# Gated linear attention and MLP on one core: decay rows stored with head pairs innermost, g loaded as rows, first q scaled ahead of k

## The chip, the cores and the metric

The kernel runs on one core of a Trainium2 chip. The core has a matrix engine (TensorE, PE in the profile, with PEld for its weight loads), a vector engine (VectorE, DVE), an activation engine (ScalarE, ACT), a general engine (GpSimd, POOL) and SyncE (SP), which here does little but issue DMAs. Each engine runs its own list of instructions in order and waits on semaphores for the others. The metric is device time in microseconds (us) from launch to end; smaller is better.

## The reference

The inputs are q, k, v and alpha, each with 4 batches, 8 heads, 768 tokens and 48 features per head, and the MLP's g_ln, w_ch1 and w_ch2. The first half is a recurrence per head:

```python
for t in range(S):
    state = alpha[:, :, t, :, None] * state + np.einsum('bhd,bhe->bhde', k[:, :, t], v[:, :, t])
    y[:, :, t] = np.einsum('bhd,bhde->bhe', q[:, :, t], state)
```

The heads are then laid side by side into rows of 384, and the second half is an MLP with a residual:

```python
xn = (x - mu) / np.sqrt(var + 1e-06) * g_ln
out = x + np.maximum(xn @ w_ch1, 0.0) @ w_ch2
```

w_ch1 is 384 x 1536 and w_ch2 1536 x 384, both given as 8-byte floats, which the kernel rounds to 4 bytes itself.

## The kernel before, in words

The 768 tokens are cut into 6 chunks of 128. For each chunk c and batch b, `attention(c, b)` replaces the loop over tokens by matrix products. With L the running sum of log(alpha) within a block, q is multiplied by exp(L) and k by exp(-L); the scores are then an ordinary masked product of q and k, and the state is carried from block to block by a factor exp(L at the block's last token), one number per head and feature. The code calls these factors the gates. In chunk 0 a block is the whole 128 tokens (one row of gates), later it is a half of 64 (two rows).

The steps of one `attention`, with the names of the profile:

- L341, ACT: `la` = Ln(alpha). L346 (chunk 0) and L353 (later), PE: `lps` = running sum, a product with a triangle of ones from `consts`.
- L356, ACT: `eq` = Exp(lps). L357, ACT: `lps` = Exp(-lps), in place.
- L359, DVE: the k half of `qk` = k * lps. L361, DVE: the q half of `qk` = q * eq.
- L367, SP: the last row (or the two last rows) of `eq` goes to a DRAM tile `row`, 512 numbers a row. L461, SP: `row` is read back into `gate`, so that the numbers of one row lie one below the other, feature by partition, with one column for each of the 4 pairs of heads. L479 (DVE, chunk 0) and L485 (POOL, later) multiply the state by `gate`.
- L413, PE: `qk` is transposed, k first, then q (from step 12 of 24 on a DVE block transpose and DMAs do it instead); L417 copies. L426/L441, PE: scores `aps`. L450/L455, DVE: masked copy into `at`. L470, PE: `ups`, the update of the state. L496/L506, PE: outputs `yps`.
- L515 to L566: layer norm without g, and its transpose `xT`.

In `eq` of before, the free order is pair of heads, head of the pair, feature (64 places, 48 used): `[P, NP, 2, 64]`. A row in DRAM has that order too, so in the read at L461 the 4 pairs of one feature lie 128 numbers apart:

```python
nc.sync.dma_start(gate[:, :ne], row[:ne].rearrange("o (p r) -> r o p", p=NP))
```

The MLP: `g_ln` is folded into w_ch1. Each of 8 weight pieces is staged (`ws`) and rounded by `round_weights`: DVE L250, L252, L254, then ACT L256, then DVE L260, and for w_ch1 three L263, which multiply by the column `g_col` of `small`. For the first piece ACT also scales `g_col` by 2^-20 (L258). `g_col` is loaded by an ACT-issued DMA (L220) from g_ln, viewed as 128 partitions by 3 columns. Chunk 0 goes through the plain products L589 (`hidden`) and L601 (`project`); chunks 1 to 5 through products of sums of blocks (L892, L713), whose sums DVE and POOL make (L695, L836, L861, L666 and others).

The order of all this is written out by hand: each attention step, weight piece, product and sum is a generator, and `ORDER` (L28) is a string of letters, each of which advances one generator by one `yield` (L963). Instructions go to the engines in exactly that order; nothing reorders them. The DMAs of SP go out in their order too, and SP stops at a DMA that must wait. Before the string begins there are loads of `consts` (ACT) and alpha (SP), memsets, and 8 matmuls on zeros (L286) in a PSUM bank named `idle`.

Of the kernel before, what the change touches and what calls it, by code (L numbers as in the profile page):

```python
# [9 lines left out]
FP32 = mybir.dt.float32  # L10
# [4 lines left out]
AOP = mybir.AluOpType  # L15
# [40 lines left out]
def pick(marks, usual=0):  # L56
    return int(marks.pop(0)) if marks else int(usual)
# [3 lines left out]
def kernel(  # L61
# [36 lines left out]
    nc = tc.nc  # L98

    B, S, H, D = q.shape  # L100
    DM = H * D
    DF = w_ch1.shape[1]
    P = 128
    NCB = S // P
    NP = H // 2
    R = 64 + D
    NF = DM // P
# [4 lines left out]
    cpool = ctx.enter_context(tc.tile_pool(name="const", bufs=1))  # L112
# [11 lines left out]
    r = np.arange(P)  # L124
# [3 lines left out]
    raws = {}  # L128
# [80 lines left out]
    tri, ident = consts[:, :P], consts[:, P:2 * P]  # L209
# [8 lines left out]
    w2_src = w_ch2.rearrange("(j p) m -> p j m", p=P)  # L218
    with nc.allow_non_contiguous_dma(reason="one small column load"):
        nc.scalar.dma_start(g_col, g_ln.rearrange("(f p) -> p f", p=P))  # L220

    pieces = []
# [16 lines left out]
    def round_weights(i):  # L239
# [11 lines left out]
           op0=AOP.bitwise_and, op1=AOP.bitwise_or)  # L251
# [4 lines left out]
        nc.scalar.activation(out=lo, in_=lo, func=AFT.Relu, scale=8.0, bias=least)  # L256
        if i == 0:
            nc.scalar.mul(g_col, g_col, 2.0 ** -20)  # L258
        yield
# [21 lines left out]
    more = cpool.tile([P, 4, NJ // 3 * DM // 2], FP32, name="more")  # L281
    zero = more.rearrange("p i m -> p (i m)")[:, 20 * P:21 * P]
    nc.vector.memset(zero, 0.0)
    idle = ps.tile([P, 512], FP32, name="lps", tag="bank", bufs=6)
    for _ in range(8):
# [6 lines left out]
    shared = more.rearrange("p i m -> p (i m)")[:, :4 * NP * P]  # L292
    eqs = [cpool.tile([P, NP, 2, 64], FP32, name=f"eq{b}") for b in range(2)]
    eqs += [shared[:, i * NP * P:(i + 1) * NP * P].rearrange(
        "p (a b c) -> p a b c", b=2, c=64) for i in range(2)]
    qks = [cpool.tile([P, 2, NP, 2, 64], FP32, name=f"qk{b}") for b in range(3)]
    qks.append(shared[:, 2 * NP * P:].rearrange("p (i a b c) -> p i a b c", i=2, b=2, c=64))
    sts = [[cpool.tile([R, NP, D], FP32, name=f"st{b}_{i}") for i in range(2)] for b in range(B)]
    for b in range(B):
        nc.vector.memset(eqs[b].rearrange("p a b c -> p (a b) c")[:, :, D:], 0.0)  # L300
        nc.vector.memset(qks[b].rearrange("p i a b c -> p (i a b) c")[:, :, D:], 0.0)
# [3 lines left out]
    def eq_of(c, b):  # L305
        return eqs[b if c < 2 else b % 2]
# [11 lines left out]
    for u in updates:  # L318
        nc.vector.memset(u, 0.0)

    x_of, xT_of, hT_of, las, turned_of, scores = ({} for _ in range(6))

    def attention(c, b):
# [12 lines left out]
        qk = qk_of(c, b).rearrange("t n p i c -> t n i p c")[:, :, :, :, :D]  # L338
        eq = eq_of(c, b).rearrange("t p i c -> t i p c")[:, :, :, :D]
        la = work.tile([P, 2, NP, D], FP32, name="la", tag="row", bufs=8)  # L340
# [7 lines left out]
        else:  # L348
# [9 lines left out]
        yield  # L358
        nc.vector.tensor_mul(qk[:, 1], raws.pop(("k", c, b)), lv)  # L359
        yield  # L360
        (nc.vector, nc.gpsimd)[pick(marks)].tensor_mul(  # L361
            qk[:, 0], raws.pop(("q", c, b)), eq)
        ends = slice(P - 1, P) if whole else slice(HS - 1, P, HS)
        ne = 1 if whole else 2
        row = dram.tile([2, 2 * 64 * NP], FP32, name="row", tag="row")
        gate = work.tile([P, 2, NP], FP32, name="gate", tag="gate", bufs=B)
        nc.sync.dma_start(row[:ne], eq_of(c, b)[ends].rearrange("o p i c -> o (p i c)"))  # L367
        yield
# [91 lines left out]
        with nc.allow_non_contiguous_dma(reason="two rows to columns"):  # L460
            nc.sync.dma_start(gate[:, :ne], row[:ne].rearrange("o (p r) -> r o p", p=NP))  # L461
        yield
# [157 lines left out]
    def buffers_of_last():  # L620
# [7 lines left out]
        late_of["h"] = [t.rearrange("p (j b t) -> p j b t", b=HB, t=P) for t in h]  # L628
        sums = [t.rearrange("t p i c -> t (p i c)") for t in eqs[:2]]
        sums += [more_x[:, NT * HB * P:]] + [t[:, 512:] for t in free]  # L630
# [363 lines left out]
```

## Time and profile before

| | |
|---|---|
| median of 3 runs | 419.09 us (417.46 to 420.03) |
| profiled execution | 418.39 us |
| its span, first to last instruction | 416.6 us |
| PE busy | 410.1 us, 98% |
| DVE, ACT, POOL busy | 292.3, 217.3, 120.4 us |
| mean share of the 16 DMA engines, SP's queue | 56.7% |
| DMA packets, and those under 512 B | 134445, 90956 |
| L361 q * eq, L356 Exp, each 24 times | 0.55 and 0.49 us each |

The profile is of one execution; the 1.8 us between its time and its span lie outside the first and last instruction. "PE busy" includes the time in which a matmul is stretched by the next one's wait, so 98% is not a peak; the chain of waits tells which engine the end hangs on. A row of the timeline gives start, duration, engine, line, what is written and read, and in brackets how long the engine was idle before it and who ended that. In a table by windows, each engine has its busy time and its number of instructions, followed by the granted clock, the DMA share and the GB/s.

### The profile page before, as it was taken

The page shows a single profiled execution, that of the slowest core. Times are in us where ns is not written, and L with a number is a line of the kernel's source. Part 1 is how long each engine was busy: PE and PEld are TensorE (multiplying, and loading weights), DVE is VectorE, ACT ScalarE, POOL GpSimd, SP SyncE. Part 2 cuts the span into 40 slices and gives each one's busy share as a digit, 9 for nine tenths or more (in the row PEclk, how much of TensorE's full clock was granted, in tenths as well). Part 3 has the DMA queues.
Part 4 walks back from the last instruction along what each step waited for, and adds up shares of the span by engine and source line. Part 5 has one row for each costly group of instructions (what it writes and reads, how often), then busy time and mean ns, then how long its engine had stood idle before and what let it go on. Part 6 is the DMA issues. An engine that isn't in the chain of part 4 may idle for free.

```text
span 416.6 us, 11452 instructions
## 1 busy us (share of the span) xinstructions
PE 410.1 (98%) x4616; PEld 355.0 (85%) x4616; DVE 292.3 (70%) x554; ACT 217.3 (52%) x522; POOL 120.4 (29%) x134
## 2 busy tenths in 40 slices
PE   7999999999999999999999999999999999999997
PEld 5887888876568789998889998899998889999996
DVE  4797989998997878688268983579533298115754
ACT  4798568773364577245585335873353643245110
POOL 1011023130011562144470254260236321525300
PEclk9999999999999999999999999999999999999999
DMA  7998968788878576945767758636323200000301
GB/s 249 289 258 258 298 155 289 206 196 211 245 156 240 154 133 141 244 100 121 186 135 160 191 160 211 116 61 132 108 57 119 72 1 2 19 0 23 111 20 57
DMA packets 134445, 61.26 MB, mean 147 GB/s; under 512 B 90956, under 2 KB 131276, under 8 KB 134392
## 3 DMA queue, kind: packets, MB, share of 16 engines
q1 hardware_dynamic: 133848, 60.37, 56.7%
q8 instruction: 36, 0.59, 0.6%
q10 hardware_dynamic: 544, 0.17, 0.2%
q14 instruction: 17, 0.14, 0.1%
HBM read 43.12 MB, written 17.39 MB: 145 GB/s over the span
## 4 chain that ended last, share of the span: by engine, by line
PE 94%; DMA 2%; DVE 1%; ACT 1%; issue 1%; SPq 0%; DVEq 0%
PE hps L892 32%; PE ops L713 31%; PE hps L589 8%; PE ops L601 8%; PE yps L506 5%; PE aps L441 3%; PE tps L413 2%; PE ups L470 2%; PE lps L353 2%; DMA ra<-in_alpha_dram 2%; PE aps L426 1%; PE yps L496 1%; DVE eq L861 1%; PE xps L564 1%; SPq L166 0%
## 5 line engine op out<-in xcount | busy, mean ns | idle before, releaser
L892 PE MATMUL hps<-sum,w 128*128 128x256 f32 x192 | 46.3, 383 | 0.0
L892 PEld LDWEIGHTS hps<-sum,w 128*128 128x128 f32 x192 | 35.6, 190 | 6.3 <-ACT u L904 1.7
L713 PE MATMUL ops<-w,hT 128*128 128x192 f32 x224 | 40.5, 326 | 0.0
L737 ACT COPY u<-ops 128x192 f32<-128x192 f32 x30 | 9.5, 317 | 54.3 <-PE ops L713 54.2
L713 PEld LDWEIGHTS ops<-w,hT 128*128 128x128 f32 x224 | 37.3, 190 | 0.3
L733 POOL TENSOR_TENSOR ob<-ob,u 128x192 f32<-128x192 f32 x32 | 20.4, 648 | 57.3 <-ACT u L737 33.0
L485 POOL TENSOR_TENSOR mid<-mid,gate 112x192 f32<-112x192 f32 x20 | 13.2, 660 | 79.5 <-DMA gate<-row 47.5
L589 PE MATMUL hps<-xT,w 128*128 128x256 f32 x144 | 33.9, 385 | 0.2 <-ACT few L537 0.2
L892 PE MATMUL hps<-xT,w 128*128 128x256 f32 x136 | 33.3, 380 | 0.6 <-DVE xT L861 0.6
L904 ACT COPY u<-hps 128x512 f32<-128x512 f32 x32 | 18.7, 586 | 28.6 <-PE hps L892 22.4
L601 PE MATMUL ops<-w,hT 128*128 128x384 f32 x96 | 32.6, 491 | 0.0
L589 PEld LDWEIGHTS hps<-xT,w 128*128 128x128 f32 x144 | 26.2, 190 | 4.2 <-ACT few L537 0.4
L904 ACT COPY hT<-hps 128x512 f32<-128x512 f32 x40 | 23.3, 586 | 12.3 <-PE hps L892 11.9
L892 PEld LDWEIGHTS hps<-xT,w 128*128 128x128 f32 x136 | 25.7, 190 | 4.3 <-PE ops L713 0.9
L713 PE MATMUL ops<-ws,sum 128*128 128x192 f32 x160 | 28.6, 327 | 0.0
L601 PEld LDWEIGHTS ops<-w,hT 128*128 128x128 f32 x96 | 17.7, 190 | 11.7 <-issue 0.6
L713 PEld LDWEIGHTS ops<-ws,sum 128*128 128x128 f32 x160 | 26.4, 190 | 0.7 <-ACT few L537 0.6
L727 DVE TENSOR_TENSOR ob<-ops,ob 128x192 f32<-128x192 f32 x40 | 13.1, 350 | 16.9 <-PE ops L713 10.4
L931 ACT ACTIVATE hT<-hT 128x512 f32<-128x512 f32 x40 | 22.9, 621 | 2.0 <-DVE hT L911 1.5
L713 PE MATMUL ops<-ws,hT 128*128 128x192 f32 x128 | 23.4, 326 | 0.0
L713 PE MATMUL ops<-more,sum 128*128 128x192 f32 x120 | 22.2, 328 | 0.0
L713 PEld LDWEIGHTS ops<-ws,hT 128*128 128x128 f32 x128 | 21.3, 190 | 0.1
(223 smaller groups left out, 1029.3 us busy)
## 6 DMA issues: line engine op xcount, KB each, us to landing
ws<-in_moe_w_ch_dram SPq DMA_DIRECT2D x8, 1152.0 KB
vn<-in_v_dram SPq DMA_DIRECT2D x12, 384.0 KB
kept<-x SPq DMA_DIRECT2D x24, 192.0 KB
ob<-kept SPq DMA_DIRECT2D x24, 192.0 KB
rows<-rj SPq DMA_DIRECT2D x48, 96.0 KB
out_dram<-ob SPq DMA_DIRECT2D x18, 192.0 KB
xrows<-xt SPq DMA_DIRECT2D x64, 48.0 KB
xT<-xrows SPq DMA_DIRECT2D x16, 192.0 KB
```

Source lines behind the costliest of these rows:

```text
L441: nc.tensor.matmul(pair[o][halves[i if o else 1 - i], p, s], k_of[rs, p, s], q_of[rs, p, s], start=True, stop=True)
L485: nc.gpsimd.tensor_mul(new, new, by)
L506: nc.tensor.matmul(yps[j][halves[s], i, p], of, by, skip_group_check=True, start=not (cross and k), stop=k == 1 or not cross)
L589: nc.tensor.matmul(hps, w1[:, f, j * P:(j + 1) * P], xT_of[0][:, f, bs], start=(f == 0), stop=(f == NF - 1))
L601: nc.tensor.matmul(ops_of[b], hT_of[c][:, j, b], w2[:, j], start=(j == 0), stop=(j == NJ - 1))
L713: nc.tensor.matmul(acc, lhs[:, j], rhs[:, j], start=j == 0 and n not in FOLLOWS, stop=j == NT - 1 and n not in FOLLOWS.values(), skip_grou ...
L727: nc.vector.tensor_add(x, acc, x)
L733: getattr(nc.vector if c + 1 == NCB else nc.gpsimd, f"tensor_{op}")(x, x, y)
L737: copy(out=copied[n], in_=acc)
L892: nc.tensor.matmul(acc[:, i], w, b, start=n not in JOINS and i == 0, stop=n not in JOINS.values(), skip_group_check=True)
L904: nc.scalar.copy(out=copied[n], in_=acc)
L931: nc.scalar.activation(out=x, in_=x, func=AFT.Relu)
```

## The change

There are three edits.

1. `eq` is laid out as `[P, 2, 64, NP]`: the 4 pairs of heads are innermost. Exp (L356) writes it with a step of 4 numbers between features, and the q product (L361) reads it so. The row in DRAM has the same order, and the read into `gate` takes the 4 pairs of a feature as 16 consecutive bytes. The built program has `gate<-row` as 128 x 4 (chunk 0) and 128 x 2 x 4 (later), where before it was 128 x 4 x 1 and 128 x 8 x 1.
2. g_ln is loaded as 3 rows of 128 into a free part of `more`, transposed on PE into the `idle` bank, and copied to `g_col` by a DVE instruction, which also does the scaling by 2^-20. The column load and the ACT instruction L258 are gone.
3. In the first attention step alone, q * eq is issued on DVE ahead of k * lps.

```diff
-    with nc.allow_non_contiguous_dma(reason="one small column load"):
-        nc.scalar.dma_start(g_col, g_ln.rearrange("(f p) -> p f", p=P))
...
-        if i == 0:
-            nc.scalar.mul(g_col, g_col, 2.0 ** -20)
...
+    g_row = more.rearrange("p i m -> p (i m)")[:NF, 21 * P:22 * P]
+    nc.scalar.dma_start(g_row, g_ln.rearrange("(f p) -> f p", p=P))
     nc.vector.memset(zero, 0.0)
...
-    eqs = [cpool.tile([P, NP, 2, 64], FP32, name=f"eq{b}") for b in range(2)]
+    eqs = [cpool.tile([P, 2, 64, NP], FP32, name=f"eq{b}") for b in range(2)]
...
+    nc.tensor.transpose(idle[:, P:P + NF], g_row, ident[:NF, :NF])
+    nc.vector.tensor_scalar(out=g_col, in0=idle[:, P:P + NF], op0=AOP.mult, scalar2=None,
+                            scalar1=1.0 if w_ch1.dtype == FP32 else 2.0 ** -20)
...
-        eq = eq_of(c, b).rearrange("t p i c -> t i p c")[:, :, :, :D]
+        eq = eq_of(c, b).rearrange("t i c p -> t i p c")[:, :, :, :D]
...
-        nc.vector.tensor_mul(qk[:, 1], raws.pop(("k", c, b)), lv)
-        yield
-        (nc.vector, nc.gpsimd)[pick(marks)].tensor_mul(
-            qk[:, 0], raws.pop(("q", c, b)), eq)
+        def scale(n):
+            if n:
+                nc.vector.tensor_mul(qk[:, 1], raws.pop(("k", c, b)), lv)
+            else:
+                (nc.vector, nc.gpsimd)[pick(marks)].tensor_mul(
+                    qk[:, 0], raws.pop(("q", c, b)), eq)
+
+        first = c + b == 0
+        scale(not first)
+        yield
+        scale(first)
...
-        nc.sync.dma_start(row[:ne], eq_of(c, b)[ends].rearrange("o p i c -> o (p i c)"))
+        nc.sync.dma_start(row[:ne], eq_of(c, b)[ends].rearrange("o i c p -> o (i c p)"))
...
-            nc.sync.dma_start(gate[:, :ne], row[:ne].rearrange("o (p r) -> r o p", p=NP))
+            nc.sync.dma_start(gate[:, :ne], row[:ne].rearrange("o (r p) -> r o p", p=NP))
```

In the built program the lists of the engines are otherwise the same. PE gets the transpose of g between the first two L346, with a wait for the load of g; DVE gets the copy ahead of the first two products of the first step. The first L263 waited for DVE and for ACT; now it waits for DVE alone.

More of the change, by code (lines that the diff above doesn't have):

```diff
@@ L292 @@
     shared = more.rearrange("p i m -> p (i m)")[:, :4 * NP * P]
-    eqs = [cpool.tile([P, NP, 2, 64], FP32, name=f"eq{b}") for b in range(2)]
+    eqs = [cpool.tile([P, 2, 64, NP], FP32, name=f"eq{b}") for b in range(2)]
     eqs += [shared[:, i * NP * P:(i + 1) * NP * P].rearrange(
-        "p (a b c) -> p a b c", b=2, c=64) for i in range(2)]
+        "p (b c a) -> p b c a", b=2, c=64) for i in range(2)]
     qks = [cpool.tile([P, 2, NP, 2, 64], FP32, name=f"qk{b}") for b in range(3)]
@@ L299 @@
     for b in range(B):
-        nc.vector.memset(eqs[b].rearrange("p a b c -> p (a b) c")[:, :, D:], 0.0)
+        nc.vector.memset(eqs[b][:, :, D:].rearrange("p b c a -> p b (c a)"), 0.0)
         nc.vector.memset(qks[b].rearrange("p i a b c -> p (i a b) c")[:, :, D:], 0.0)
@@ L628, in buffers_of_last @@
         late_of["h"] = [t.rearrange("p (j b t) -> p j b t", b=HB, t=P) for t in h]
-        sums = [t.rearrange("t p i c -> t (p i c)") for t in eqs[:2]]
+        sums = [t.rearrange("t i c p -> t (i c p)") for t in eqs[:2]]
         sums += [more_x[:, NT * HB * P:]] + [t[:, 512:] for t in free]
```

## The prediction

> **What bounds the kernel now.** I read the page's busy times and chain of waits first, then the chain piece by piece for where it leaves PE, then the windows and timeline of those places.
>
> ```profile
> PE 410.1 (98%) x4616; PEld 355.0 (85%) x4616; DVE 292.3 (70%) x554; ACT 217.3 (52%) x522; POOL 120.4 (29%) x134
> PE 94%; DMA 2%; DVE 1%; ACT 1%; issue 1%; SPq 0%; DVEq 0%
> ```
>
> The end hangs on PE for 94% of the span, so an edit elsewhere pays only where the chain leaves PE. From the chain in order of time:
>
> ```profile
> 2.63 6.41 DMA ra<-in_alpha_dram
> 9.07 0.53 ACT la L341
> 9.60 0.04 issue
> 9.64 1.56 PE lps L346 x4
> ```
>
> Up to 9.64 us the end hangs on a load: the alpha of the third step lands at 9.04 us, its Ln follows, and from the L346 at 9.64 us PE has work without a break until 28.0 us. There the chain passes through ACT until the first MLP product at 32.84 us; from then to 333.6 us it stays on PE. The last break, 333.6 to 339.3 us, is DVE sums of chunk 5, which no edit touches. So two places count: the start, and 28 to 33 us.
>
> **Part by part. g as rows.** The windows of the start (us; each engine's busy time and count; clock; DMA share; GB/s):
>
> ```profile
> 2.70:3.70 1.00, 1.00 (x6) 1.00 (x6) 0.42 (x2) 0.10 (x1) 0.00 (x0) 1.00 1.11 348
> 3.70:4.70 1.00, 1.00 (x7) 1.00 (x6) 0.00 (x0) 0.43 (x1) 0.00 (x0) 1.00 0.73 58
> 4.70:5.70 1.00, 1.00 (x3) 0.26 (x2) 0.00 (x0) 0.30 (x1) 0.00 (x0) 1.00 0.71 189
> 5.70:6.70 1.00, 1.00 (x2) 0.50 (x2) 0.00 (x0) 0.78 (x3) 0.00 (x0) 1.00 1.02 376
> ```
>
> The reader is to see the hole: 58 and 189 GB/s between 3.7 and 5.7 us, with 348 before and 376 to 396 behind, while the loads of alpha, k and q were queued throughout. In just that time the 384 4-byte packets of g run on ACT's queue (the packet records show them from 2.9 to 5.4 us). The hole is (390 - 58) + (390 - 189) = 533 KB, 1.4 us at 390 GB/s. If g is not its cause, the gain is only what g's packets occupy: 384 x 9 ns / 16 engines = 0.2 us. Bounds 0.2 and 1.4; I take 1.0, nearer to the hole, since hole and packets coincide. With g as three 512-byte rows, alpha of step 1 (landed 5.4), k (7.5), q (8.5) and alpha of step 2 (9.04) come 1.0 us earlier.
>
> What is late next? The first L346 runs from 4.62 us behind the zero products, unchanged. The second started at 5.98; its alpha is now early, but PE passes the transpose of g first: one pass, by the zero products beside it 0.24 us. (It waits for three rows queued behind `consts`, which landed at 3.8, so they should be there.) Lps of step 1 thus ends about 0.15 us later, and with it ACT's four Exp: 8.5 instead of 8.33 us. The Ln of step 2, ready at 8.05, waits for them, ends at 9.05, and its L346 can start at 9.1 instead of 9.64. The DVE copy of g (some 0.2 us, by L534's 0.197 for one column) lies in DVE's idle time before 7.59. Gain at the start, **0.5 us**: of 1.0 us in arrivals, ACT's Exp eat half.
>
> **First q ahead of k.** Now DVE takes k, then q:
>
> ```profile
> 7.59 0.56 DVE L359 TENSOR_TENSOR qk<-rk,lps 128x384 f32<-128x384 f32 x1 [4.46 <-DMA rk<-in_k_dram]
> 8.55 0.56 DVE L361 TENSOR_TENSOR qk<-rq,eq 128x384 f32<-128x384 f32 x1 [0.40 <-DMA rq<-in_q_dram]
> ```
>
> Both wait for loads, and q lands last. In the new order k stands behind q's landing: q 7.55 to 8.1, k to 8.65, then the transposes of k on PE (four of 0.11) to 9.15. The L346 of step 2 stands behind these on PE and wants 9.1: cost under 0.1 us, within the 0.5. If the loads do not come earlier, it is 8.55 + 2 x 0.55 + 0.5 = 10.15 against 9.64, a loss of 0.5 (second rival).
>
> **L258 goes, and L263 loses a wait.** DVE and PE's weight loads between 29 and 36 us, and the same DVE step of the second piece (no bracket: no idle time before it):
>
> ```profile
> 30.19 1.36 DVE L260 SCALAR_TENSOR_TENSOR ws<-ws 128x1152 int32<-128x1152 int32 x1 [0.23 <-ACT ws L256]
> 32.07 1.68 DVE L263 SCALAR_TENSOR_TENSOR w<-w,small,ws 128x384 f32<-128x384 f32 x3 [0.52 <-ACT xT L566]
> ...
> 46.80 1.68 DVE L263 SCALAR_TENSOR_TENSOR w<-w,small,ws 128x384 f32<-128x384 f32 x3
> ```
>
> ```profile
> 33.27 0.30 PEld L589 LDWEIGHTS hps<-xT,w 128*128 128x128 f32 x2 [0.17 <-DVE w L263]
> 33.80 2.24 PEld L589 LDWEIGHTS hps<-xT,w 128*128 128x128 f32 x11 [0.23 <-DVE w L263]
> ```
>
> The first L263 stands 0.52 us idle after L260, the second one 0.03: only the first waits for two engines. PE's first MLP products wait for exactly these three L263 (0.17 and 0.23 us above): 18 products take 4.25 us where 18 x 0.216 = 3.89 is their pace, and start 0.2 us after the work before them. All of it is DVE's lateness. With the wait for ACT gone, L263 starts at about 31.6, and PE gets back 0.3 to 0.56 us; I take **0.45**, the idle time less the 0.03 and a little for PE's own work, which ends at 32.64. That ACT is spared L258 (0.19 us) comes on top of slack and is counted at nothing.
>
> **Gates in 16-byte pieces.** 4 x 512 + 20 x 1024 = 22528 elements become 5632 pieces, so packets fall to 134445 - 16896 - 381 = 117168 and those under 512 B to 90956 - 16896 - 384 = 73676. The ring is really freed: where the first two gates are read, 15.7 to 17.7 us, the windows show 154 and 96 GB/s. But who waits? From 33 to 310 us the lists of waits of PE and of its weight loads name no DMA, and POOL, which waits for gates (47.5 us in 5 waits), is off the chain: of the PE products that read POOL's state, the closest starts 0.4 us after it. I cost it at nothing; the cover is PE's own work. Bounds are 0 and a gain of 3 us: the weight loads' waits for other engines there sum to 6.1 us, and half of them I take to lie beside matmuls.
>
> **Exp and q product with a step of 16 bytes.** No row of the trace has this step. Nearest are the rows on 8-byte words, of which one half is touched. On DVE, L260 takes 1.36 us for 1152 elements; by the slope from L727 (192: 0.350) to L361 (384: 0.548), 1.03 ns each, it would be 1.34. So no surcharge. On ACT, L256 takes 1.36; by L931 (512: 0.618) and 0.84 ns each (L737 to L904) it would be 1.16, a sixth more. For 384 elements that is 0.06 us. Lower bound nothing (a gain is excluded: same elements, same engines); upper bound twice the time per element: +0.40 us for each of 24 L361 and +0.32 for each L356. I take DVE 0, ACT 0.06, by the nearest rows; DVE is at 98% in 50 to 60 us, so this is where a cost would bite (first rival).
>
> The Trainium skill, "SBUF — State Buffer", section "Specifications (TRN2)", speaks against this edit: it gives SBUF lines of 16 bytes, needs at least two hits per line for full bandwidth, and says that each crossing to a new line pays. Here every element is in a new line; in the 8-byte rows two share one. The page gives no size; no run yet shows any. By it the sum would be that of the first rival.
>
> **Sum.** 418.39 - 0.5 - 0.45 = 417.4 us for the profiled execution, span 415.6. That execution lies 0.7 us under the median of its runs, so the median goes from 419.09 to **418.1 us**, 0.2% faster. About 1% is what a measurement of this kernel can tell from no change; this is well inside.
>
> **Rivals.**
>
> 1. *The 16-byte step doubles the time per element; slower.* Against: the 8-byte rows. For: nothing in them crosses a line at each element. A lead, below, is the start of a PE product less the end of the DVE instruction that it waits for. Place: steps 0 and 1 (two Exp, +0.64, push the Ln of step 2 past its gain: the 0.5 is lost), then PE waits for DVE where its lead is short. The third q product ends 0.15 us before PE needs it (15.61): +0.25. Two q products before the transpose at 24.36, lead 0.6: +0.2. At 28 to 33 us one more Exp ahead of L256 takes 0.32 of the 0.45. At 47.9 us PE's lead over L263 is 0.45, and two q products make DVE about 0.55 late: +0.1. From 50 us on leads of 0.9 to 4 us and DVE's idle gaps take up the rest. Sum -0.13 + 0.55 = +0.4: median 419.5. It decides from a surcharge of about 0.2 us an instruction on. If the surcharge were three times that of doubling, DVE becomes the bound from 20 to 100 us (10 q products of 1.2 us more, against 6.3 us in which DVE is idle there and 1 to 2 us of lead): +4 to +5 us, median 423 to 424. That tail I hold for unlikely.
> 2. *The hole is not g's.* For: the loads then only begin. Against: the coincidence, and 348 GB/s before it. The start then loses 0.5 (k behind q), L263 gives 0.45: median 419.1.
> 3. *The freed ring pays.* For: DMA shares of 1.0 from 5 to 30 and 40 to 50 us. Against: PE has hardly a wait there to give back. At most all of 3 us more: 415.1.
> 4. *The gates do not come in 16-byte pieces*: excluded by the built program's shapes; it would cost nothing that the sum has counted.
>
> **Chances.** Forecast 0.60, first rival 0.22 (0.03 of it the tail), second 0.10, third 0.08. The tail is the only case over 1% slower; a little is added for what no row shows: slower by over 1% 0.05, faster by over 1% 0.03 (414.9 needs the whole third rival), within 1% 0.92. Range: from the third rival's middle, 416.1, to the first rival's 419.5, widened to the 1.0 to 1.6 us by which three runs of one kernel lay apart from their median: 415.9 to 420.7.
>
> **What the new profile would show.** Windows 3.7 to 5.7 us at over 300 GB/s; the Ln of step 2 at 8.5 and its L346 at 9.1 us. First L263 right behind L260, the first 18 products in under 4.0 us. 117168 packets. L356 at 0.49 to 0.55 and L361 at 0.55 us. PE's chain otherwise the same. The forecast is wrong if L361 or L356 is above 0.7 us, if the hole stays, or if PE waits for DVE between 15 and 100 us where it now doesn't.

## The result, and the profile after

The changed kernel takes 421.73 us (median of 12 runs, 419.99 to 423.48), the kernel before in the same comparison 419.26 us (12 runs, 417.36 to 420.14). The ratio is 1.0072, with a 95% interval of 1.0052 to 1.0091: 0.7% slower. (The ratio is an estimate from the runs of both kernels and not the quotient of the two medians, which is 1.0059; the same holds below.) The forecast was 418.1 us, 0.2% faster, with a range up to 420.7. The profiled execution took 423.43 us, one of the longest of the twelve, and its span is 421.6 us; the profile of before is of a shorter execution than most. So the two traces lie further apart (5.0 us) than the medians (2.5 us).

The page of the changed kernel: busy time of each engine, the chain by engine, and the packets.

```profile
PE 413.1 (98%) x4617; PEld 356.1 (84%) x4617; DVE 299.2 (71%) x555; ACT 225.0 (53%) x521; POOL 122.6 (29%) x134
PE 93%; DMA 2%; DVE 2%; ACT 1%; issue 1%; SPq 0%; DVEq 0%
DMA packets 117155, 61.26 MB, mean 145 GB/s; under 512 B 73663, under 2 KB 113986, under 8 KB 117102
```

DVE and ACT have 6.9 and 7.7 us more of work than before, and PE is still the engine on which the end hangs. The packets are those forecast (117168) but for 13.

Where the added DVE and ACT time lies, the rows of the two lines that work on the new layout show (count, then shortest, median and longest in ns). L365 is the q product (L361 before), L358 the Exp (L356 before).

```profile
L365 DVE TENSOR_TENSOR qk<-rj,eq x12: 845/866/1393, 85.9 to 267.9; 128x384 f32<-128x384 f32 x12
L365 DVE TENSOR_TENSOR qk<-rq,eq x8: 842/855/901, 8.0 to 71.6; 128x384 f32<-128x384 f32 x8
```

```profile
L358 ACT ACTIVATE eq<-lps x20: 836/866/905, 6.2 to 265.6; 128x384 f32<-128x384 f32 x20
```

Before, the same 384 elements took 0.55 us on DVE and 0.49 us on ACT. Each of 24 q products now costs 0.31 us more, each of 24 Exp 0.375 us more: 0.8 and 1.0 ns an element. The second Exp, behind it on ACT and without the step, takes 0.60 us in place of 0.49, but the records of the two overlap by 0.2 us, so ACT's busy time grows by 0.32 us a step (7.7 / 24).

The start, by windows (us; busy time and count of PE, PEld, DVE, ACT, POOL; clock; DMA share; GB/s):

```profile
3.70:4.70 1.00, 1.00 (x7) 1.00 (x6) 0.00 (x0) 0.81 (x2) 0.00 (x0) 1.00 1.12 333
4.70:5.70 1.00, 1.00 (x3) 0.26 (x2) 0.00 (x0) 0.23 (x1) 0.00 (x0) 1.00 0.85 284
9.00:11.00 2.00, 1.66 (x6) 1.21 (x7) 2.00 (x4) 0.50 (x1) 0.00 (x0) 0.70 1.06 380
11.00:13.00 2.00, 2.00 (x6) 1.10 (x5) 0.45 (x2) 1.23 (x2) 0.00 (x0) 0.50 0.99 296
```

In this trace the hole in the loads is gone: 333 and 284 GB/s where 58 and 189 stood. But the granted clock of PE, full throughout this stretch in the profile of before, is 0.70 and 0.50 from 9 to 13 us, and the mean clock is below 0.998 in 11 of the 12 executions. The chain of the changed kernel in order of time (start, us, what), pieces of its start and one near 139 us:

```profile
2.11 5.77 DMA rq<-in_q_dram
...
8.15 0.59 issue
8.75 0.55 DVE qk L363
9.35 0.74 PE tps L422 x4
10.09 2.56 PE lps L348 x4
...
138.95 3.92 DMA kT<-rows
```

The end now hangs on q's load, on the k product behind it (L363), and on k's transposes at 9.35 us; they started at 8.20 before. PE had been idle for 2.15 us ahead of them. The four products of step 2 behind them take 2.56 us at the lower clock, 1.56 us before. Near 139 us PE waits for a DMA where it did not.

The two traces can be laid side by side by the order of PE's products. The distance by which the changed kernel is behind is 0.24 us at 9.9 us, 1.4 us at 12.4 (the clock), 2.5 us at 24, 2.75 at 50, 3.3 at 103, 4.8 at 143 (1.25 us of it at the wait for kT), and 5.0 us from 238 us on. From 15 us on it grows almost only in short steps, each at a single pair of products.

### The profile page after: what moved, and what is told of

Same layout as the page of the kernel before. It is cut to its first block, busy times and chain, and to the rows that moved or that the text cites. A ratio compares the mean times of both kernels' runs of the same rounds, so it can differ in the third digit from the quotient of the medians.

```text
span 421.6 us, 11452 instructions
## 1 busy us (share of the span) xinstructions
PE 413.1 (98%) x4617; PEld 356.1 (84%) x4617; DVE 299.2 (71%) x555; ACT 225.0 (53%) x521; POOL 122.6 (29%) x134
## 4 chain that ended last, share of the span: by engine, by line
PE 93%; DMA 2%; DVE 2%; ACT 1%; issue 1%; SPq 0%; DVEq 0%
PE hps L901 31%; PE ops L722 30%; PE ops L610 8%; PE hps L598 7%; PE yps L515 4%; PE ups L479 3%; PE tps L422 2%; PE aps L450 2%; PE lps L355 2%; DMA rq<-in_q_dram 1%; PE aps L435 1%; PE yps L505 1%; DMA kT<-rows 1%; PE xps L573 1%; DVE eq L870 1%
## 5 line engine op out<-in xcount | busy, mean ns | idle before, releaser
L742 POOL TENSOR_TENSOR ob<-ob,u 128x192 f32<-128x192 f32 x32 | 21.4, 679 | 57.8 <-ACT u L746 46.4
L494 POOL TENSOR_TENSOR st<-st,gate 112x192 f32<-112x192 f32 x16 | 15.6, 972 | 27.7 <-DVE st L492 27.7
L722 PE MATMUL ops<-ws,hT 128*128 128x192 f32 x128 | 23.5, 327 | 0.1
```

Of the source, the lines that this page charges most:

```text
L494: nc.gpsimd.tensor_mul(new, new, by)
L722: nc.tensor.matmul(acc, lhs[:, j], rhs[:, j], start=j == 0 and n not in FOLLOWS, stop=j == NT - 1 and n not in FOLLOWS.values(), skip_grou ...
L742: getattr(nc.vector if c + 1 == NCB else nc.gpsimd, f"tensor_{op}")(x, x, y)
```

## The experiments

Ratios are to the kernel before, measured on the same chip beside each run, with 95% intervals. "Edit 1" is the layout with the gates, "edit 2" g as rows, "edit 3" q first.

### One edit at a time

Edit 1 alone is every line of the diff that touches `eq`, `row`, `gate` or `sums`:

```diff
-    eqs = [cpool.tile([P, NP, 2, 64], FP32, name=f"eq{b}") for b in range(2)]
+    eqs = [cpool.tile([P, 2, 64, NP], FP32, name=f"eq{b}") for b in range(2)]
...
-            nc.sync.dma_start(gate[:, :ne], row[:ne].rearrange("o (p r) -> r o p", p=NP))
+            nc.sync.dma_start(gate[:, :ne], row[:ne].rearrange("o (r p) -> r o p", p=NP))
```

> The kernel before with the new layout alone (16-byte step in Exp and in the q product, gates in 16-byte pieces); g by column, k first. Theory A (the step of 16 bytes is the cost: 0.87 us for each Exp and 0.86 for each q product, as in the changed kernel's profile): slower than before by 1.0 to 2.5 us, with no drop of the granted clock between 9 and 13 us, since k's product is not held behind q. Theory B (the clock is the cost: PE idle from 7.2 to 9.35 us because k's product stands behind q's, then 0.50 to 0.70 of the clock until 13 us): within 0.5 us of before. Theory C (the load of g as rows did it): within 0.5 us.

Measured: 420.46 us, ratio 1.0052 (1.0020 to 1.0083).

Edit 2 alone:

```diff
+    g_row = more.rearrange("p i m -> p (i m)")[:NF, 21 * P:22 * P]
+    nc.scalar.dma_start(g_row, g_ln.rearrange("(f p) -> f p", p=P))
...
+    nc.tensor.transpose(idle[:, P:P + NF], g_row, ident[:NF, :NF])
```

> The kernel before with g loaded as rows and turned, nothing else. By the prediction's sum: -0.95 us. Theory A and B: the same gain, 0.5 to 1.2 us faster, the hole of 3.7 to 5.7 us filled, the first L263's 0.52 us of idle time gone. Theory C: as slow as the changed kernel, +2.5.

Measured: 417.72 us, ratio 0.9996 (0.9968 to 1.0023). Its profiled execution has a span of 415.1 us and is 1.2 us ahead of before at the first MLP product and 1.5 us at 146 us; the median of the runs does not confirm that gain. Single traces differ by such amounts in any case. There are pauses of PE that the profile puts to no releaser (0.9 us at 21 us with edit 1 alone, 0.5 us near 43 us here), and the trace of before is 0.8 us slow near 142 us in a place where this one and nine others are not.

Edit 3 alone:

```diff
-        nc.vector.tensor_mul(qk[:, 1], raws.pop(("k", c, b)), lv)
-        yield
-        (nc.vector, nc.gpsimd)[pick(marks)].tensor_mul(
-            qk[:, 0], raws.pop(("q", c, b)), eq)
+        first = c + b == 0
+        scale(not first)
+        yield
+        scale(first)
```

> The kernel before with the first q product ahead of k, nothing else. q lands at 8.5 us here, so the transposes of k come at about 9.7 instead of 8.2 and PE is idle from 7.4 to 9.7. Theory A: +0.5 us (the L346 of step 2 behind these transposes). Theory B: +0.5 and the clock falls to about half from 9.5 to 13 us, another 1.3: +1.8 us in all.

Measured: 419.84 us, ratio 1.0029 (1.0005 to 1.0054). The mean granted clock of an execution was below 0.998 in 7 of its 12 runs (median 420.64 us) and above in 5 (418.66 us).

The gates alone: before, with the read of the gates as 16 consecutive bytes and nothing else changed (the rows keep their order, so the gates land in other places).

```diff
-            nc.sync.dma_start(gate[:, :ne], row[:ne].rearrange("o (p r) -> r o p", p=NP))
+            nc.sync.dma_start(gate[:, :ne], row[:ne].rearrange("o (r p) -> r o p", p=NP))
```

> The kernel before, but the gates are read as 16 consecutive bytes out of the old row, so the gates stand in wrong places (the states and outputs are other numbers); no step in Exp or in the q product. It shows what the larger pieces are worth by themselves. By the prediction nothing: within 0.4 us of before, though packets fall to about 117500 and POOL waits less for gates. By its third rival the freed ring pays: 1 to 3 us faster.

Measured: 417.28 us, ratio 0.9987 (0.9968 to 1.0007).

What follows: 0.52 - 0.04 + 0.29 = 0.77%, and the whole change has 0.72%. The three edits add up, within their intervals; the layout carries about two thirds of the loss, q first the rest. The DMA pieces are worth between nothing and 0.3%, so the layout's loss is not theirs.

### Two edits at a time

Edits 2 and 3:

> The changed kernel with the old layout: g as rows and q first. Theory A: as g_only, -0.9 us. Theory B: q at 8.0, then k, transposes at about 9.1, PE idle for 1.9 us; if that is long enough for the clock to fall, +0.3 to +1.0 against before, if it is not, -0.9. The difference of the changed kernel less this one is the price of the layout behind the other two edits: 2 to 3.5 us by A, under 1 by B.

Measured: 419.29 us, ratio 1.0020 (0.9999 to 1.0040).

Edits 1 and 2, with k first as before:

> The changed kernel with k ahead of q again in the first step: new layout and g as rows. Theory A+B (two prices that add: the 16-byte step some 2.2 us, as the layout alone measured, and q first 1.2 us through PE's idle time and the clock): 1.0 to 2.0 us over before, the clock at 1.00 from 9 to 13 us in nearly all runs, so 1 to 2 us faster than the changed kernel. Rival (the step of 16 bytes is all, and q first is absorbed behind it): as slow as the changed kernel, 2.5 to 3.0 over before.

Measured: 419.67 us, ratio 1.0040 (1.0024 to 1.0056). So on top of edit 2 the layout costs 0.44% (0.52% alone), and q first 0.24% (0.29% alone): within the intervals the order of the sum does not matter.

Edits 1 and 2 differ from edit 2 alone by the layout, and both profiled executions have a full granted clock, so their traces show where the layout's loss arises. DVE's masked copy of the scores and PE's weight loads of the MLP near 66 us, from the timeline (start, us, engine, line; in brackets the idle time before). Edit 2 alone:

```profile
65.60 0.72 DVE L457 COPY_PREDICATED at<-consts,aps 128x512 f32<-128x512 int32 x1
66.00 1.70 PEld L591 LDWEIGHTS hps<-xT,w 128*128 128x128 f32 x8
66.48 0.54 DVE L363 TENSOR_TENSOR qk<-rq,eq 128x384 f32<-128x384 f32 x1
```

Edits 1 and 2:

```profile
66.63 0.72 DVE L457 COPY_PREDICATED at<-consts,aps 128x512 f32<-128x512 int32 x1
67.46 1.16 PEld L591 LDWEIGHTS hps<-xT,w 128*128 128x128 f32 x6 [0.43 <-PE hps L591]
67.50 0.85 DVE L363 TENSOR_TENSOR qk<-rq,eq 128x384 f32<-128x384 f32 x1
```

With edit 2 alone the copy is done at 66.32 us and the weight loads run through it without a break. With the layout DVE is a further microsecond behind, the copy is done at 67.35 us, and the next weight load starts 0.11 us later, behind a wait for DVE that stands in PE's queue there. The list of waits has no row for it, because the matmul ahead is shown as stretched over the gap: this is a loss in a stretch in which "PE busy" is 100%.

The same comparison over the whole trace: where the distance from one product's start to the next grows by over 0.2 us for good.

| at (us, edit 2 alone) | next product | edit 2 alone | edits 1 and 2 |
|---|---|---|---|
| 14.70 | tps, transposes of a step | 0.12 | 0.38 |
| 23.45 | tps | 0.11 | 0.32 |
| 31.57 | hps, first MLP product | 0.11 | 0.38 |
| 47.03 | hps | 0.15 | 0.39 |
| 66.43 | hps | 0.22 | 0.44 |
| 99.10 | ops | 0.32 | 0.54 |
| 232.17 | ops | 0.16 | 0.37 |

The seven sum to 1.6 us; the spans differ by 416.8 - 415.1 = 1.7 us, the ratios to before by 0.44%, 1.8 us. That the first two sums meet is partly luck: with the layout the trace also gains 0.2 us near 9 us and 0.7 us at 42.6 us (the pause of edit 2 alone is missing), and steps smaller than these seven take about as much away. What does not hang on one trace are the places: the waits at 14.7, 66, 99 and 232 us are in all four traces with both 16-byte steps in every one of the 24 steps, and not in those of before, of edit 2 alone and of the gates alone. The changed kernel has such steps at five of these places too (17.3, 50.2, 70.0, 102.9 and 238.4 us in its own time), each of 0.2 to 0.3 us.

### What in the layout costs

Only a step of 8 bytes: two pairs of heads innermost, the other two outside, so that two elements of one instruction share 16 bytes. The row then goes to DRAM in two DMAs. This is on top of edit 2.

```diff
-    eqs = [cpool.tile([P, 2, 64, NP], FP32, name=f"eq{b}") for b in range(2)]
+    eqs = [cpool.tile([P, 2, NP // 2, 64, 2], FP32, name=f"eq{b}") for b in range(2)]
...
-        nc.sync.dma_start(row[:ne], eq_of(c, b)[ends].rearrange("o i c p -> o (i c p)"))
+        for h in range(2):
+            nc.sync.dma_start(row[:ne].rearrange("o (h i x) -> o h i x", h=2, x=P)[:, h],
+                              eq_of(c, b)[ends][:, :, h].rearrange("o i c l -> o i (c l)"))
```

> g as rows, k first, and another layout: only two pairs of heads innermost, so Exp and the q product step by 8 bytes and gates return in 8-byte pieces; each row is stored by two DMAs in place of one. If the cost lies in every element being in a new 16-byte line, the step of 8 bytes is free or nearly so: Exp at 0.49 to 0.55 and q product at 0.55 us, and the time is that of g as rows alone, 0.4 to 1.0 us under before. If any step costs, by half: Exp about 0.68, q product about 0.70, and 0 to 0.7 us over before.

Its rows of the q product:

```profile
L363 DVE TENSOR_TENSOR qk<-rj,eq x12: 541/552/1075, 83.9 to 265.4; 128x384 f32<-128x384 f32 x12
```

and of the Exp:

```profile
L358 ACT ACTIVATE eq<-lps x20: 503/520/550, 5.8 to 263.0; 128x384 f32<-128x384 f32 x20
```

At a step of 8 bytes the instructions cost what they cost without one (0.55 and 0.49 us), but for 0.03 us on ACT. With 16 bytes, when every element lies in new 16 bytes, the surcharge is there. The Trainium skill, "SBUF — State Buffer", section "Specifications (TRN2)", says just this (lines of 16 bytes, at least two hits in each for full bandwidth), and the trace agrees: two hits cost nothing on DVE and 0.03 us on ACT, one hit +0.31 and +0.375 us for 384 elements. Only steps of 4, 8 and 16 bytes were run, so a limit of another kind between 8 and 16 bytes would fit these numbers as well as lines do.

Yet the time was 421.40 us, ratio 1.0077 (1.0050 to 1.0105). The suspect was its 24 further DMA issues on SP. To measure them by themselves: edit 2 alone, in the layout of before, with each row stored in two halves.

```diff
-        nc.sync.dma_start(row[:ne], eq_of(c, b)[ends].rearrange("o p i c -> o (p i c)"))
+        for h in range(2):
+            nc.sync.dma_start(row[:ne, h * 2 * P:(h + 1) * 2 * P],
+                              eq_of(c, b)[ends][:, 2 * h:2 * h + 2].rearrange("o p i c -> o (p i c)"))
```

> Edit 2 alone, and each row of exp(L) stored by two DMAs of half its length, in the layout of before: 24 DMA issues of SP more, as in the run with the 8-byte step. If these issues, and the loads behind them on SP that come later, are what made that run slow: ratio to the kernel before 1.004 to 1.008 (419.5 to 421.2 us), with kT landing 1 to 2 us late near 139 us. If not, 0.998 to 1.001 as edit 2 alone, and the loss of that run stays with its layout.

Measured: 422.01 us, ratio 1.0102 (1.0077 to 1.0127), against 0.9996 without the second issue. From its chain:

```profile
51.22 0.52 SPq L370
...
51.78 0.49 SPq L370
...
52.38 7.84 DMA ws<-in_moe_w_ch_dram
```

Each issue holds SP for 0.5 us. Behind the two stands the load of a piece of MLP weights, issued at 52.38 us where with edit 2 alone it went at 47.28; DVE waits 1.6 us for it, and the chain runs through it. The chain of the run with the 8-byte step runs through the same load, issued at 52.03 us. So the issues alone explain what that run lost; what that layout would be worth with one DMA a row was not tried.

Which engine's surcharge matters? Edit 1 with the 16-byte step in one instruction only; the other one works on the same tile with the pairs outside. (These two runs, and the three by steps below, also clear all of `eq` at the start instead of its unused places.) First the Exp alone:

```diff
         (nc.vector, nc.gpsimd)[pick(marks)].tensor_mul(
-            qk[:, 0], raws.pop(("q", c, b)), eq)
+            qk[:, 0], raws.pop(("q", c, b)),
+            eq_of(c, b).rearrange("t i c p -> t (i c p)").rearrange(
+                "t (p i c) -> t i p c", p=NP, i=2)[:, :, :, :D])
```

> Edit 1 with the 16-byte step in ACT's Exp alone: Exp writes exp(L) with the pairs innermost, the q product reads the same tile as if the pairs stood outside, so that its 48 elements of a head are next to one another. The q products thus read other gates than the reference's; nothing is left out and every wait stays. Expected of the instructions: Exp 0.85 to 0.87 us, q product 0.55. Theory S, that both surcharges are on the path about as they are long: 0.375 of 0.685 of the layout's price of 0.5%, ratio to the kernel before 1.002 to 1.004 (419 to 419.5 us). Rival V, that only VectorE's surcharge is on the path: 0.999 to 1.001. Rival A, that only ACT's is: 1.004 to 1.006. Rival N, that the layout's price is no matter of the step: 0.998 to 1.001 here and in the run with VectorE's step alone.

Measured: 419.07 us, ratio 1.0018 (0.9995 to 1.0041). And the q product alone:

```diff
-        nc.scalar.activation(out=eq, in_=lv, func=AFT.Exp)
+        nc.scalar.activation(
+            out=eq_of(c, b).rearrange("t i c p -> t (i c p)").rearrange(
+                "t (p i c) -> t i p c", p=NP, i=2)[:, :, :, :D],
+            in_=lv, func=AFT.Exp)
```

> Edit 1 with the 16-byte step in VectorE's q product alone: Exp writes the tile with the pairs outside, the q product reads it with the pairs innermost. The q products again read other gates than the reference's, nothing is left out. Expected of the instructions: Exp 0.49 us, q product 0.845 to 0.87. Theory S: ratio to the kernel before 1.0015 to 1.0035. Rival V: 1.004 to 1.006. Rival A: 0.999 to 1.001. Rival N: 0.998 to 1.001.

Measured: 419.29 us, ratio 1.0027 (1.0010 to 1.0043). Without either step (the run of the gates alone) nothing is lost, and with DVE's step alone something is. That ACT's step alone costs is not shown: its interval includes no loss, and among executions whose mean clock is at least 0.998 its median is that of before (418.02 and 418.06 us), where DVE's step is at 419.01. In the same count the whole layout is 2.4 us over before (420.27 and 417.90), more than the two added up; how far the steps act together stays open. In the traces, with places in the time of before, the waits at 15.6, 24.4 and 233.8 us appear with DVE's step alone and not with ACT's, that at 67.3 us with ACT's and not with DVE's. At 100.1 us the distance is 0.32 us before and with ACT's step, 0.41 with DVE's and 0.54 with both.

In which of the 24 steps? Edit 1 with the 16-byte step in some steps only:

```diff
         eq = eq_of(c, b).rearrange("t i c p -> t i p c")[:, :, :, :D]
+        if not (c == 0):
+            eq = eq_of(c, b).rearrange("t i c p -> t (i c p)").rearrange(
+                "t (p i c) -> t i p c", p=NP, i=2)[:, :, :, :D]
```

> Edit 1 with the 16-byte step (Exp and q product) in the first four of the 24 steps alone; in the other twenty both write and read the tile with the pairs outside, so their gates come from wrong places of the row; nothing is left out. Theory F, that the layout costs at the start, where Ln, lps, Exp and the products are one chain (edit 1 alone lost 1.6 us between 16 and 33 us): ratio 1.003 to 1.005 of the 1.0052 of edit 1 alone. Rival E, that each of the 24 steps pays alike: 1.000 to 1.0015.

Measured: 418.39 us, ratio 0.9998 (0.9974 to 1.0023). The same with `c == 1`:

> Edit 1 with the 16-byte step in the second four of the 24 steps alone (17 to 32 us); in the others Exp and the q product write and read the tile with the pairs outside, so their gates come from wrong places of the row; nothing is left out. Theory G, that the price is paid where edit 1 alone lost 1.6 us in its trace, between 16 and 33 us, and the first four steps have been found to pay nothing: ratio 1.002 to 1.004. Rival E, that every step behind the first four pays alike: a fifth of 0.5%, 0.999 to 1.0015.

Measured: 417.89 us, ratio 0.9982 (0.9960 to 1.0003). The same with `c > 0`:

> Edit 1 with the 16-byte step in the last twenty of the 24 steps alone, the first four with the pairs outside (their gates from wrong places of the row). Theories G and E alike: 1.004 to 1.006, all that edit 1 alone costs. Rival L, that the price is no sum over the steps and needs the first ones too: 0.999 to 1.002.

Measured: 420.48 us, ratio 1.0029 (1.0003 to 1.0055). The first four steps lose nothing that can be measured, and neither do the second four: the theory that the loss between 16 and 33 us in the trace of edit 1 alone (one gap of PE of 1.0 us at 21 us) was its price fell. By subtraction the price is in the last sixteen steps, but the last run is below what either theory gave, its interval reaches from nearly nothing to all of it, and the table above puts three of seven waits before 32 us. Nor is a wait bound to the steps near it: with the step in the second four alone, done by 32 us, the distance at 100.1 us is 0.47 us. How the price divides over the steps stays open.

### What in the order of q and k costs

The changed kernel with ten more products of zeros on PE ahead of the first transposes of k, so that PE is not idle there:

```diff
+        for _ in range(10 if c + b == 0 else 0):
+            nc.tensor.matmul(updates[1].rearrange("r p d -> r (p d)")[:, :P], zero[:, :R], zero,
+                             start=True, stop=True)
         for i in () if turned(c, b) else (1, 0):
```

> The changed kernel with ten more products on zeros on PE ahead of the first transposes of k (into a bank that is overwritten later), which fill PE's idle time from 7.2 to 9.3 us. Theory B: the clock stays at 1.00 from 9 to 13 us and the time falls by 1.3 to 2.0 us against the changed kernel, to 1.0 to 1.7 over before. Rival (the idle time itself is the cost, not the clock): no faster than the changed kernel, 2.5 to 3.0 over before.

Measured: 422.11 us, ratio 1.0093 (1.0069 to 1.0117); clock full in all 6 runs, and no time gained. The same on edit 3 alone:

> Edit 3 alone, and ten more products of zeros on PE ahead of the first transposes of k, which run while PE waits for k. Theory C, that q first costs what it does because PE is idle for 2 us, its granted clock falls to about half for 3 us, and the late start is carried on: the granted clock is 1.00 between 9 and 13 us in every run, and the time falls from the 419.8 of edit 3 alone to 418.2 to 418.9 (ratio to the kernel before 1.000 to 1.0015). Rival K, that the loss is that k and all behind it come later, and the clock only goes with it: clock 1.00 as well, the ratio stays 1.002 to 1.004.

Measured: 420.41 us, ratio 1.0052 (1.0024 to 1.0080), clock full in all 10 runs. Its profiled execution, the longest of the ten, had regained the late start (0.4 us ahead of before at 32 us), and then met this in its chain:

```profile
40.49 1.43 issue
```

a pause of PE in which it waits for nothing that the profile shows, and one of 1.0 us near 216 us. Neither is in the kernel before; the second is at the same product in both traces with ten more products, and in no other. Ten instructions more are thus no clean test, so the next one adds none: of the eight zero products at the start four are issued ahead of k's transposes instead.

```diff
-    for _ in range(8):
+    for _ in range(4):
         nc.tensor.matmul(idle[:, :P], zero, zero, start=True, stop=True)
...
+        for _ in range(4 if c + b == 0 else 0):
+            nc.tensor.matmul(updates[1].rearrange("r p d -> r (p d)")[:, :P], zero[:, :R], zero,
+                             start=True, stop=True)
```

> Edit 3 alone; of the eight products of zeros at the start four are issued ahead of the first transposes of k instead, so PE has as many instructions as before and its idle time there falls from 2 to 1 us. Theory C, that half of the loss is the fall of the granted clock behind an idle time of 2 us: dips in no more than a fifth of the runs, ratio 1.000 to 1.002 (edit 3 alone: 1.0029, dips in 7 of 12). Rival K, that k's lateness alone makes the loss: 1.002 to 1.004 with or without dips.

Measured: 418.32 us, ratio 1.0015 (0.9993 to 1.0037), clock above 0.998 in all 12 runs. (In its trace PE's idle time has moved to 3.1 us, where it lasts 1.27 us.) Windows 9 to 13 us of edit 3 alone:

```profile
9.00:11.00 2.00, 1.63 (x6) 1.33 (x7) 1.74 (x4) 0.74 (x2) 0.00 (x0) 0.52 1.07 379
11.00:13.00 2.00, 2.00 (x8) 1.12 (x7) 0.51 (x2) 0.87 (x2) 0.00 (x0) 0.62 1.06 357
```

and with four products moved:

```profile
9.00:11.00 2.00, 1.97 (x8) 1.52 (x8) 1.63 (x4) 0.48 (x1) 0.00 (x0) 1.00 1.06 381
11.00:13.00 2.00, 2.00 (x17) 1.51 (x15) 0.92 (x2) 1.46 (x3) 0.00 (x0) 1.00 1.08 352
```

The fall of the clock is caused by the idle PE: with the gap filled it is gone, and PE gets through 17 products between 11 and 13 us in place of 8. The ratio goes half way back, but the intervals overlap. Among executions at a clock of at least 0.998 alone, edit 3 is 0.8 us over before (418.66 in 5 executions, 417.90 in 25), and so is this run (418.32 in 12, 417.50 in 28). That points to k's lateness for some 0.8 us, and to the clock for the rest of the 1.2 us; with so few executions it is an estimate.

Is it the order of the products, or the wait for the second load? Before, with only the two first loads exchanged:

```diff
-        for n, src in (("a", alpha), ("k", k), ("q", q)):
+        first = (("q", q), ("k", k)) if c + m == 0 else (("k", k), ("q", q))
+        for n, src in (("a", alpha), *first):
```

> The kernel before, with one thing changed: SP issues the first load of q ahead of the first load of k; k is still multiplied and turned first. Theory W, that q first costs because the first k product then waits for the second of the two loads (8.5 us in place of 7.6) and PE is idle for 2 us ahead of it: the same loss appears here without any change in the order of the products: ratio to the kernel before 1.002 to 1.004, granted clock below 0.998 in about half of the runs. Rival P, that the order of the products itself costs (k's transposes behind q's product on VectorE): 0.999 to 1.001 here.

Measured: 418.05 us, ratio 0.9996 (0.9968 to 1.0024); clock below 0.998 in 4 of 12 runs. And edit 3 with the loads exchanged and q turned first, the mirror of before:

```diff
-        for i in () if turned(c, b) else (1, 0):
+        for i in () if turned(c, b) else (0, 1) if c + b == 0 else (1, 0):
```

> Edit 3, with the first load of q issued ahead of k's and step 1's q turned ahead of its k, so that the start is that of before with the names of q and k exchanged. Theory W: no loss is left, ratio 0.999 to 1.001, dips of the granted clock in about a fifth of the runs, as in the kernel before. Rival P: 1.002 to 1.004 as in edit 3 alone.

Measured: 417.87 us, ratio 1.0011 (0.9989 to 1.0033), clock below 0.998 in 2 of 12. The mirror loses nothing that can be measured, and gains nothing, so q first as such is free; it costs when the loads and the transposes stay in the old order. The exchange of the loads alone was expected to lose as edit 3 does and did not: in its trace k's product starts at 7.99 us, 0.40 later than before, and k's transposes at 8.60; in edit 3 alone at 9.37, since there k's product stands behind the load of q and behind q's product as well.

No version here with every gate in its place beats the kernel before: edit 2 alone and the exchange of the loads, the nearest, are at 0.9996.

## Why the prediction was wrong

**Exp and q product with a step of 16 bytes: the mis-sized term.** The sum has "DVE 0, ACT 0.06" for each, taken from rows with an 8-byte step. Measured: +0.31 and +0.375. The 8-byte rows were right about 8 bytes (0.55 and 0.52 us in the run with that step) and say nothing of 16; the text itself noted that two elements share 16 bytes there. The rule of the Trainium skill that it set beside them, from "SBUF — State Buffer", section "Specifications (TRN2)", was the better guide. With the bounds from nothing to +0.40 and +0.32 it had the size inside for DVE and just missed it on ACT; the choice of the nearest row in place of the far bound is what failed.

**The first rival's price.** Its mechanism is what happened: PE waits for DVE where the lead is short. At about its surcharge it gave +0.4 us over before, that is 1.4 us over the forecast; the layout measures +0.44 to 0.52%, about 2 us. Its list had places near 15.6, 24.4, 28 to 33 and 48 us, and these are in the table (14.7, 23.5, 31.6, 47.0), at 0.2 to 0.3 us each. What failed is "from 50 us on leads of 0.9 to 4 us and DVE's idle gaps take up the rest": three more waits of 0.2 us are at 66, 99 and 232 us. Leads were looked up for the q product's own readers, but DVE works in order: the masked copy at 66 us and a DVE sum at 232 us stand behind q products in its queue, and in the kernel before PE's next weight load starts 0.1 and 0.16 us after they end. The rival also reckoned from a gain of 0.95 us that the runs do not show. With what was measured in place of the forecast's terms (edit 2 nothing, the layout 1.8 to 2.2 us, q first 1.0 to 1.2) the sum is 2.8 to 3.4 us over before; 0.72% is 3.0.

**First q ahead of k: "cost under 0.1 us, within the 0.5".** Measured +0.24% on edit 2, +0.29% alone, 1.0 to 1.2 us. The loads did come earlier, but q's product starts at 7.98 us, not 7.55, and takes 0.84, not 0.55; k's transposes start at 9.35, not 8.65. The error in time is 0.7 us. What the step left out altogether is what an idle PE does to its clock.

**g as rows: 0.5 + 0.45.** Only a part of the hole was g's, and the 1.0 us in arrivals is mis-sized. The trace of before is the emptiest of all: from 3.7 to 5.7 us it moves 247 KB (58 + 189), the twelve other traces with g by column 310 to 473 KB (mean of the thirteen 373), the seven with rows 480 to 691 (mean 566). Edit 3 alone, by column, and edits 1 and 2, by rows:

```profile
3.70:4.70 1.00, 1.00 (x7) 1.00 (x6) 0.00 (x0) 0.52 (x1) 0.00 (x0) 1.00 0.82 219
4.70:5.70 1.00, 1.00 (x3) 0.26 (x2) 0.00 (x0) 0.52 (x1) 0.00 (x0) 1.00 0.88 217
...
3.70:4.70 1.00, 1.00 (x7) 1.00 (x6) 0.00 (x0) 0.92 (x2) 0.00 (x0) 1.00 0.88 270
4.70:5.70 1.00, 1.00 (x5) 0.44 (x4) 0.00 (x0) 0.18 (x2) 0.00 (x0) 1.00 0.76 210
```

So g by column costs the loads some 190 KB, 0.5 us at 390 GB/s, and the second rival was half right. The first L258 (L263 before) stands right behind L255, as forecast, in the timeline of the changed kernel:

```profile
33.09 1.36 DVE L255 SCALAR_TENSOR_TENSOR ws<-ws 128x1152 int32<-128x1152 int32 x1 [0.35 <-ACT ws L253]
34.48 1.68 DVE L258 SCALAR_TENSOR_TENSOR w<-w,small,ws 128x384 f32<-128x384 f32 x3
```

But the 18 products behind it take 4.29 us, not under 4.0 (4.15 with edit 2 alone). L255 ahead of them still waits for ACT, 0.35 us in the row above and 0.23 before; with edit 3 alone, whose Exp are no longer than before, it is 0.35 us too, so the cause is open. Nor is it shown that the wait ahead of L263 went with the old L258: it is missing, and 0.36 us is gained at the first MLP product, in the trace of edit 2 alone, but the same in that of edit 3 alone and in others that keep the column and the ACT instruction. In the trace of edit 2 alone a gain of 1.2 us stands at 32 us; in the median of 12 runs it is 0.0 us, give or take 1.1. A gain of 0.95 us is within that and so is none.

**Gates in 16-byte pieces: nothing.** Right: -0.13% (-0.32 to +0.07%). The third rival is out.

**"The lists of waits name no DMA from 33 to 310 us."** True of before, and no cover: its last kT landed at 138.13 us, 0.2 us ahead of the first product that reads it. In the changed kernel, with edit 3 alone and with edits 2 and 3, PE loses 0.7 to 1.3 us there.

**What would show it wrong** was named rightly: L361 and L356 above 0.7 us, and PE waiting for DVE between 15 and 100 us; both came true.

## What to carry to other kernels

A layout that makes a DMA better but gives an engine's instruction one element in every 16 bytes lengthened every such instruction here, by half on DVE and three quarters on ACT, and it buys nothing if nobody waits for the DMA. In a kernel whose PE is 98% busy, a list of waits without DVE does not say that DVE is off the path: look up, for each wait in PE's queue, how long the releasing instruction had been done, and count everything behind the slowed instruction in its engine's order. Before a hole in one trace is priced, look at the same windows in a second trace: here it was the deepest of thirteen. When two consumers are exchanged, exchange the loads and what reads the results with them.

## What the runs showed of the hardware

- **The clock falls after short idle times of PE.** In four profiled executions the granted clock was half for 3.41 us. PE had been idle for 2.15 us (the changed kernel), 2.71 us (edit 3 alone), 1.78 us (the loads exchanged), and for 0.98 and 0.78 us in short order (the step in the last twenty steps). With 2.37 us (edits 2 and 3) it stayed full, as it did with idle times like the last in most other traces. Half the clock for 3.41 us takes 0.004 off the mean over 417 us, and 0.996 is what most executions below 0.998 show. There are 11, 7, 4 and 4 of 12 such executions for the kernels with 2.15, 2.71, 2.37 and 1.78 us, so their share does not follow the length; 58 of 267 for the kernel before and those without such a gap; none of 28 for the three with the gap filled. Within one kernel such executions are longer, by 2.0 us for edit 3 alone and by 1.4 to 3.2 us for the kernel before, by chip. The half clock itself can take no more than 1.7 us (half of 3.41), so it is not the whole of every such difference. The Trainium skill, "TensorE: Matmul & The Clock Gate", section "Why this matters for your kernels", warns of gaps of over about 3 us; here 2 us were enough in about half of the executions.
- **An SP issue is not free.** 24 more issues of 0.5 us each cost 1.0% where a load of weights stood behind them.
- **PE pauses without a releaser.** Ten more matmuls on an idle PE came with pauses of 1.4 and 1.0 us at other places, of which the profile names no cause; traces without them have such pauses too (0.9 us with edit 1 alone, 0.7 us with edits 2 and 3). It stays open what they are.
